# Decode attention beside a feed-forward branch, one core: the first weight load is split by partitions

## The chip, the cores and the metric

The kernel runs on one core of a Trainium2 chip. The metric is the device time of one execution in microseconds. The kernel before took 695.85 us (median of 3 runs, 695.55 to 696.01). One more execution was recorded by the hardware profiler; all rows shown are of that one.

## The reference

Two tokens (batch 2, one query position, width 640) go through two branches. Branch A is attention over a cache of 4096 positions with 32 heads of 128; branch B is a feed-forward layer of width 1728 with SiLU. A gate of each token mixes them. All is float32.

```python
def _A_ref(x, k_cache, v_cache, wq, wo):
    B, Sq, D = x.shape          # 2, 1, 640
    H, Dh = 32, 128             # caches: (2, 32, 4096, 128)
    q = (x @ wq).reshape(B, Sq, H, Dh).transpose(0, 2, 1, 3)
    scores = jnp.einsum("bhqd,bhkd->bhqk", q, k_cache) * (Dh ** -0.5)
    p = softmax(scores, axis=-1)
    o = jnp.einsum("bhqk,bhkd->bhqd", p, v_cache)
    return o.transpose(0, 2, 1, 3).reshape(B, Sq, H * Dh) @ wo

def _B_ref(x, w1, w2):          # w1 (640, 1728), w2 (1728, 640)
    h = silu(jnp.einsum("bsd,df->bsf", x, w1))
    return jnp.einsum("bsf,fd->bsd", h, w2)

g = sigmoid((x * gate_w).sum(-1, keepdims=True))
out = g * _A_ref(...) + (1 - g) * _B_ref(...)
```

## The kernel before

**Storage.** Three large areas of SBUF, the slabs `v`, `b` and `a`, hold 64 KB in each of the 128 partitions. Everything that is read in bulk passes through them: the weights of branch B and `wq` at the start, then the K and V caches, then `wo`.

**The start.** The queue of SyncE (SP in the profile) issues every transfer. Its first ones are, in this order: `w1` into slab `a` (line 303: 128 partitions, each with five whole rows of `w1`, 34,560 contiguous bytes), `x` into the tile `xs` (8 partitions), `gate` into `xs` (4 partitions), `w2` into slab `v`, `wq` into the end of `v` and all of `b` (lines 304 to 312), and a small store to the output. The issue of `x` waits for the memset of `oP_xs` on GpSimd (line 302). VectorE turns `x` and the gate row (line 420), makes a few small tiles, and then multiplies `w1` by `x` in ten steps over 1728 columns (lines 443 and 446); the first of them reads slab `a` and so waits for `w1`. TensorE sums over partitions (line 458), the SiLU follows, TensorE multiplies by `w2` (line 533) and then computes all queries from `wq` (line 608).

**The main part.** Batch and heads give 16 items of four heads each. An item has one K slab and one V slab of 8.4 MB. K goes to `a` and `b` in turn, V to `v`. For each item VectorE (line 676, columns 0 to 67) and GpSimd (line 670, the other 60) multiply K by the query in place, VectorE reduces (line 686), ScalarE takes the exponentials (line 715), TensorE multiplies them with V (line 766). The load of a K slab waits until the slab's reader before it is done, and the load of a V slab until the values of the item before are summed. The first K load (line 470, `load_k(0)`) goes into slab `a` and waits for the last VectorE step on `w1`; the first V load (line 656) and the second K load (line 657) wait for the matmuls on `wq` (line 608).

**The end.** `wo` is loaded in six pieces behind the last V slab; TensorE multiplies piece after piece (lines 556 and 586) and one store writes the result.

**Order and waits.** Every operation names the pieces it reads and writes (`part("a", 0)` is piece 0 of slab `a`, `part("a")` all eight), and the class `Flow` derives the semaphore waits from them. Each transfer has a semaphore of its own unless it names another.

Of the kernel before, what the change touches and what calls it, by code (L numbers as in the profile page):

```python
# [158 lines left out]
def gated_decode(nc, x, kc, vc, wq, wo, w1, w2, gate, out):  # L159
    P = 128  # L160
    B, H, SK, DH = kc.shape
    D = x.shape[2]
    F = w1.shape[1]
    J = D // P
# [26 lines left out]
    f = Flow(nc)  # L191
# [11 lines left out]
    slab = {n: slabs[:, k * SLAB : (k + 1) * SLAB] for k, n in enumerate("vba")}  # L203

    def part(n, *ks):
        return [f"{n}.{k}" for k in (ks or range(8))]
# [77 lines left out]
    def load_wo(g):  # L284
# [15 lines left out]


    f.op("POOL", lambda: G_.memset(oP_xs, 0.0), writes=["oP", "xs"])
    f.dma("SP", slab["a"][:, : J * F], w1.rearrange("(p j) f -> p (j f)", j=J), writes=part("a"))
    f.dma("SP", xs[0:P:HB, :], x.rearrange("b s (c n) -> (s c) b n", c=Q), reads=["xs"], writes=["xs0"])
    f.dma("SP", xs[HB // 2 : P : 32, :], gate.rearrange("(c n) -> c n", c=Q), reads=["xs"], writes=["xs1"])
    f.dma(
# [3 lines left out]
        writes=part("v", 0),  # L310
# [10 lines left out]
        writes=["ident"],  # L321
# [13 lines left out]
        writes=["block"],  # L335
# [7 lines left out]
        writes=["fold"],  # L343
# [5 lines left out]
        writes=["sel"],  # L349
# [5 lines left out]
        writes=["half"],  # L355
# [10 lines left out]
        writes=["pick"],  # L366
# [5 lines left out]
        writes=["own"],  # L372
# [5 lines left out]
        writes=["side"],  # L378
# [7 lines left out]
        writes=["spread"],  # L386
# [5 lines left out]
        writes=["mask"],  # L392
    )
    f.op("DVE", lambda: V.memset(join, 0.0), writes=["join"])
    for e in range(2):
# [7 lines left out]
            writes=["join"],  # L403
        )
        for t in (at, at + 32):
# [4 lines left out]
                writes=["join"],  # L410
# [11 lines left out]
        writes=["xt"],  # L422
# [6 lines left out]
        writes=["gx"],  # L429
# [7 lines left out]
    for b in range(B):  # L437
        for j in range(J):
# [13 lines left out]
                writes=[f"hsum{b}"],  # L452
            )

    def mm_hr():
# [19 lines left out]
        writes=["ps_o"],  # L475
# [8 lines left out]
        writes=["gc"],  # L484
# [7 lines left out]
    for e in range(2):  # L492
# [4 lines left out]
            writes=[f"spaced{e}"],  # L497
# [9 lines left out]
        writes=["he"],  # L507
    )
    for e in range(2):
# [6 lines left out]
            writes=[f"seq{e}"],  # L516
# [126 lines left out]
    for u in range(2):  # L643
        for b in range(B):
# [8 lines left out]
                writes=[f"qall{u}{b}"],  # L653
# [199 lines left out]
    for i in range(N + 1):  # L853
        j = i - 1
# [98 lines left out]
```

## Time and profile before

| what | value |
|---|---|
| median of 3 runs | 695.85 us (695.55 to 696.01) |
| the profiled execution, its own time | 695.71 us |
| its span, first to last instruction | 694.2 us |
| VectorE, GpSimd, TensorE, ScalarE busy | 507.5, 265.6, 211.4, 40.0 us |
| read from HBM | 298.26 MB |

The profiled execution's own time is 1.5 us above its span; the rest lies ahead of the first and behind the last instruction. SPq is the queue of SyncE, from which the transfers are issued; "to landing" is the time from an issue to the end of its transfer. In the rows of a time window the engines' busy times come first, then the granted TensorE clock, the busy share of the 16 DMA engines and the bytes per time. A packet is counted with its whole size where it begins, so that the share of a short window can pass 1.

### The profile page before, as it was taken

How to read it: one execution, taken by the hardware profiler on the slowest of the kernel's cores; microseconds unless marked ns; L12 is line 12 of the kernel's file. 1: busy time of each engine (PE TensorE's matmuls, PEld its weight loads, DVE VectorE, ACT ScalarE, POOL GpSimd, SP SyncE). 2: the span in 40 equal slices, each digit the busy share in tenths (PEclk: the TensorE clock that was granted, in tenths of full speed). 3: DMA queues.
4: the chain of work that ended last, by engine and by line, in shares of the span. 5: the costliest groups of instructions: out<-in, count | busy, mean ns of one | idle time of the engine just before them, and what ended most of it. 6: DMA issues, size and time to landing. Idle time of an engine off the chain costs nothing. (4 is left out here: it accounts for less than half of the span.)

```text
span 694.2 us, 3593 instructions
## 1 busy us (share of the span) xinstructions
PE 211.4 (30%) x1440; PEld 72.5 (10%) x1440; DVE 507.5 (73%) x269; ACT 40.0 (6%) x152; POOL 265.6 (38%) x26
## 2 busy tenths in 40 slices
PE   0074032151331405060412306060503315050657
PEld 0032010010110101020100101010100101010113
DVE  3810958898989596886959596986959595977811
ACT  0001010101010101010010101010000101010000
POOL 1000808191726090815335180906244270907100
PEclk9998556565565757575665757575655757575689
DMA  9999999999999999999999999999999999999997
GB/s 383 430 446 450 430 427 424 423 457 438 427 430 423 430 461 427 434 423 423 438 457 427 430 423 427 464 430 430 423 423 461 434 430 427 423 438 457 427 408 326
DMA packets 6209, 298.33 MB, mean 430 GB/s; under 512 B 672, under 2 KB 700, under 8 KB 956
## 3 DMA queue, kind: packets, MB, share of 16 engines
q1 hardware_dynamic: 6204, 298.27, 99.4%
q8 instruction: 2, 0.03, 0.0%
q14 instruction: 3, 0.02, 0.0%
HBM read 298.26 MB, written 0.01 MB: 430 GB/s over the span
## 5 line engine op out<-in xcount | busy, mean ns | idle before, releaser
L670 POOL TENSOR_TENSOR slabs<-slabs,qsb 128x7680 f32<-128x7680 f32 x16 | 262.3, 16396 | 378.7 <-DMA slabs<-in_A_k_cache_dram 347.8
L686 DVE TENSOR_REDUCE s<-slabs 128x68 f32<-128x8704 f32 (+1 forms) x32 | 276.3, 8676 | 0.0
L766 PE MATMUL ps<-slabs,pz 128*32 128x512 f32 x1024 | 146.2, 735 | 345.2 <-PEq L145 338.2
L676 DVE TENSOR_TENSOR slabs<-slabs,ps 128x8704 f32<-128x8704 f32 x16 | 147.5, 9218 | 108.5 <-DMA slabs<-in_A_k_cache_dram 108.4
L766 PEld LDWEIGHTS ps<-slabs,pz 128*32 128x32 f32 x1024 | 39.5, 132 | 438.6 <-issue 431.6
L715 ACT ACTIVATE pz<-s,nb 32x128 f32<-32x128 f32 x64 | 25.4, 398 | 556.5 <-PE ps L766 363.2
L804 PE MATMUL ps<-osb,pick 128*128 128x512 f32 x32 | 20.4, 724 | 58.9 <-PEq L145 58.0
L818 DVE TENSOR_REDUCE row<-ps 64x128 f32<-64x512 f32 x16 | 10.9, 682 | 23.3 <-PE ps L804 23.3
L788 DVE SCALAR_TENSOR_TENSOR osb<-ps,rg,own 128x512 f32<-128x512 f32 x16 | 12.0, 748 | 21.4 <-PE ps L766 21.2
L618 PE MATMUL ps<-qall,spread 128*128 (+1 forms) x32 | 7.4, 319 | 35.3 <-PEq L145 34.5
L446 DVE SCALAR_TENSOR_TENSOR slabs<-slabs 128x1728 f32<-128x1728 f32 x8 | 16.1, 2019 | 0.3
L458 PE MATMUL ps<-slabs,xz_col 128*32 128x432 f32 x16 | 3.1, 928 | 33.2 <-DVE slabs L446 33.2
L804 PEld LDWEIGHTS ps<-osb,pick 128*128 128x128 f32 x32 | 5.4, 211 | 73.0 <-issue 71.2
L715 ACT ACTIVATION_READ_ACCUMULATOR pz<-s,nb 32x1 f32 x64 | 11.8, 184 | 0.0
L618 PEld LDWEIGHTS ps<-qall,spread 128*128 128x128 f32 x32 | 6.9, 224 | 44.9 <-issue 43.2
L533 PE MATMUL ps<-slabs,seq 128*32 128x320 f32 x54 | 10.3, 545 | 3.7 <-DVE seq L512 3.7
L825 DVE STREAM_TRANSPOSE ps<-row 64x256 f32<-64x256 f32 x16 | 10.3, 642 | 0.6
L608 PE MATMUL ps<-slabs,xz_col 128*32 128x512 f32 x80 | 9.8, 593 | 0.0
L891 DVE COPY slabs<-ps 128x160 f32<-128x160 f32 x1 | 0.3, 325 | 12.2 <-PE ps L586 12.2
L556 PE MATMUL ps<-slabs,oP_xs 128*32 128x320 f32 x96 | 8.8, 433 | 1.4 <-DMA slabs<-in_A_wo_dram 1.4
L740 PE MATMUL ps<-rs,fold 128*128 128x1 f32 x32 | 6.1, 260 | 2.3 <-PEq L145 2.1
L740 PEld LDWEIGHTS ps<-rs,fold 128*128 128x128 f32 x32 | 5.7, 222 | 5.0 <-issue 3.5
(63 smaller groups left out, 71.9 us busy)
## 6 DMA issues: line engine op xcount, KB each, us to landing
slabs<-in_A_wq_dram SPq DMA_DIRECT2D x1, 10240.0 KB, 44.5
slabs<-in_B_w_dram SPq DMA_DIRECT2D x2, 4320.0 KB, 17.0
slabs<-in_A_wo_dram SPq DMA_DIRECT2D x1, 5120.0 KB, 21.5
slabs<-in_A_wo_dram SPq DMA_DIRECT2D x2, 1280.0 KB, 25.4
slabs<-in_A_wo_dram SPq DMA_DIRECT2D x1, 1600.0 KB, 30.1
slabs<-in_A_wo_dram SPq DMA_DIRECT2D x1, 640.0 KB, 31.1
slabs<-in_A_wo_dram SPq DMA_DIRECT2D x1, 320.0 KB, 31.4
slabs<-in_A_k_cache_dram SPq DMA_DIRECT2D x16, 47.8
```

The lines of the kernel that those rows point to most:

```text
L446: lambda b=b, j=j, at=at: V.scalar_tensor_tensor(hsum[:, b, :], w1t[:, j, :], at, hsum[:, b, :], op0=ALU.mult, op1=ALU.add)
L533: last = T_.matmul(early[to : to + 32, :], seq[:, k : k + 2, :].rearrange("p k z -> p (k z)"), slab[n][:, k * HD : (k + 1) * HD], start=(k ...
L618: return T_.matmul(ps_q[:, :DH], spread, qall.rearrange("p h b d -> p (h b) d")[:, i, :], start=True, stop=True,)
L670: lambda: G_.tensor_mul(k[:, CV:, :], k[:, CV:, :], qsb[:, None, :].to_broadcast([P, C - CV, DH])),
L676: lambda: V.tensor_mul(k[:, :CV, :], k[:, :CV, :], ps_q[:, None, :DH].to_broadcast([P, CV, DH])),
L686: lambda c0=c0, c1=c1: V.reduce_sum(Ss[i % 2][:, c0:c1], k[:, c0:c1, :], axis=AX.X),
L715: last = S_.activation(pz[lo:hi, :, 4 * q : 4 * q + 4], s[lo:hi].rearrange("p (g c) -> p g c", c=4), AF.Exp, bias=nb[lo:hi], scale=SCALE, ...
L740: lambda *_: T_.matmul(ps_t[:, :1], fold.rearrange("p a q c -> p (a q c)"), rs, start=True, stop=True),
L766: last = T_.matmul(ps_v[32 * q : 32 * q + 32, :], pz[:, gr, :], v[:, gr, :], start=(gr < 4), stop=(gr >= NG - 4),)
L788: lambda: V.scalar_tensor_tensor(osb, ps_v.rearrange("p (c d) -> p c d", d=DH), rg, own[:, :, None].to_broadcast([P, 4, DH]), op0=ALU.mult ...
L804: lambda *_: T_.matmul(ps_o, pick, osb.rearrange("p c d -> p (c d)"), start=True, stop=True),
L818: lambda: V.reduce_sum(row, ps_o[:64].rearrange("p (c d) -> p d c", d=DH), axis=AX.X),
```

## The change

The load of `w1` becomes two loads of the same bytes: the first takes partitions 0 to 63, the second partitions 64 to 127. Each partition still receives one run of 34,560 bytes. The first load is entered as the writer of piece 0 of slab `a`, the second as the writer of pieces 1 to 7. Both are issued from the same queue, one behind the other and ahead of `x`. The first VectorE step on `w1` reads all pieces, and so waits for two semaphores where it waited for one.

```diff
     f.op("POOL", lambda: G_.memset(oP_xs, 0.0), writes=["oP", "xs"])
-    f.dma("SP", slab["a"][:, : J * F], w1.rearrange("(p j) f -> p (j f)", j=J), writes=part("a"))
+    w1_rows = w1.rearrange("(p j) f -> p (j f)", j=J)
+    f.dma("SP", slab["a"][: P // 2, : J * F], w1_rows[: P // 2], writes=part("a", 0))
+    f.dma("SP", slab["a"][P // 2 :, : J * F], w1_rows[P // 2 :], writes=part("a", *range(1, 8)))
     f.dma("SP", xs[0:P:HB, :], x.rearrange("b s (c n) -> (s c) b n", c=Q), reads=["xs"], writes=["xs0"])
```

## The prediction

> **What bounds the kernel now.** I read the busy table first, then the DMA rows, then the chain of waits, and last the windows of the start.
>
> ```profile
> PE 211.4 (30%) x1440; PEld 72.5 (10%) x1440; DVE 507.5 (73%) x269; ACT 40.0 (6%) x152; POOL 265.6 (38%) x26
> DMA  9999999999999999999999999999999999999997
> GB/s 383 430 446 450 430 427 424 423 457 438 427 430 423 430 461 427 434 423 423 438 457 427 430 423 427 464 430 430 423 423 461 434 430 427 423 438 457 427 408 326
> q1 hardware_dynamic: 6204, 298.27, 99.4%
> HBM read 298.26 MB, written 0.01 MB: 430 GB/s over the span
> DMA 4%; PE 2%; SPq 0%; issue 0%; DVE 0%
> DMA slabs<-in_A_wo_dram 4%; PE ps L766 1%; PE ps L586 0%; SPq L69 0%; DVE slabs L891 0%
> ```
>
> No compute engine is near full; VectorE, the busiest, stands at 73%. The 16 DMA engines are busy for 99.4% of the span, in each of the 40 slices. The chain of waits follows only the last 46 us, but in those, too, the largest piece is a transfer (`wo`, 4%). The waits say the same for the main part: GpSimd, which takes up each K slab, sits idle until the slab has landed.
>
> ```profile
> POOL slabs L670 <- DMA slabs<-in_A_k_cache_dram: 347.8, 14, 64.4
> ...
> 0.00:1.70 1.70, 0.00 (x0) 0.00 (x0) 0.17 (x1) 0.97 (x1) 1.17 (x5) 1.00 0.00 0
> ...
> 67.00:667.00 600.00, 166.63 (x1052) 54.35 (x1052) 479.30 (x219) 35.33 (x143) 262.33 (x16) 0.62 1.00 433
> ```
>
> The first window is empty, and the one from 67 to 667 us, in which nearly all K and V slabs pass, has a DMA share of 1.00 at 433 GB/s. So the kernel is one long stream of 298 MB, always with something queued, and its time is bytes by rate plus a head and a tail. Two things follow. Time that the stream loses at the start is not won back later: the idle share is 0.6%, 4.2 us, and 1.7 us of that is ahead of the first packet. And moving bytes earlier or later within the stream gains nothing.
>
> **The change part by part.** The first question is how long `w1` takes now.
>
> ```profile
> 0.74 0.38 SPq L69 DMA_DIRECT2D slabs<-in_B_w_dram  x1
> 1.85 0.73 SPq L69 DMA_DIRECT2D oP_xs<-in_A_x_dram  x1
> 2.63 0.56 SPq L69 DMA_DIRECT2D oP_xs<-in_gate_w_dram  x1
> 3.23 0.43 SPq L69 DMA_DIRECT2D slabs<-in_B_w_dram  x1
> 3.71 0.43 SPq L69 DMA_DIRECT2D slabs<-in_A_wq_dram  x1
> slabs<-in_B_w_dram SPq DMA_DIRECT2D x1, 4320.0 KB, 13.1
> 1.70:12.50 10.80, 0.00 (x0) 0.00 (x0) 3.21 (x17) 0.32 (x1) 2.07 (x6) 1.00 1.02 410
> 13.48:33.20 19.72, 0.00 (x0) 0.00 (x0) 19.09 (x15) 0.00 (x0) 0.00 (x0) 1.00 1.00 431
> ```
>
> `w1` is issued at 0.74 us and lands 13.1 us later, at 13.84. It is 4320 KB, that is 4.424 MB. The window 1.70 to 12.50 moves 410 GB/s x 10.8 us = 4.43 MB: all of `w1` and next to nothing else. So `w1` holds the stream for about 10.8 us; at the settled rate of the window behind it, 431 GB/s, it would be 4.424 / 0.431 = 10.27 us, and 0.5 us are the run-up of the first packets.
>
> *The second issue.* An issue of this kind takes 0.38 to 0.43 us. SP is free from 1.12 us, and its next issue, `x`, begins only at 1.85 us, behind the memset on GpSimd:
>
> ```profile
> 0.73 1.09 POOL L302 MEMSET oP_xs<- 128x1192 f32 x1 [0.29 <-POOLq L943]
> ```
>
> 0.43 us go into that gap of 0.73 us: cost nothing. Without that cover it would move the issues of `x`, gate, `w2` and `wq` by 0.43 us, and their packets would still wait behind `w1` until about 12.5 us; nothing again.
>
> *The second wait.* The first VectorE step on `w1` (line 443) now waits for two loads. Ahead of it on VectorE stands the transposition at line 420, which waits for the gate row:
>
> ```profile
> 13.75 0.46 DVE L420 STREAM_TRANSPOSE slabs<-oP_xs 128x160 f32<-128x160 f32 x1 [7.72 <-DMA oP_xs<-in_gate_w_dram]
> 14.62 1.11 DVE L443 TENSOR_SCALAR slabs<-slabs 128x1728 f32<-128x1728 f32 x1
> 25.01 8.18 DVE L446 SCALAR_TENSOR_TENSOR slabs<-slabs 128x1728 f32<-128x1728 f32 x4
> 33.22 0.34 SPq L69 DMA_DIRECT2D slabs<-in_A_k_cache_dram  x1
> slabs<-in_A_wq_dram SPq DMA_DIRECT2D x1, 10240.0 KB, 44.5
> ```
>
> The gate row is queued behind both halves, so it stays the last to come, or lies within tenths of it. What is queued behind line 443 is the ten steps that end at 33.2 us and release the first K load at 33.22. That load then waits in the queue until `wq` has landed at 3.71 + 44.5 = 48.2 us: 15 us of cover. A second wait costs 0 within it; with the cover gone it would be some tenths.
>
> *The transfers themselves.* No load of this trace fills only half the partitions, apart from the few KB of `x` and gate, so the price must be bounded. **Low end, 0:** the rate belongs to the 16 engines, both halves are spread over all of them, and 64 partitions load as fast as 128. **High end:** the rate belongs to the destination. All bulk loads fill 128 partitions, at 431 / 128 = 3.37 GB/s for each of them; if a partition cannot take more, 64 take 215.5 GB/s. The halves then go one after the other, since one queue feeds both: 4.424 / 0.2155 = 20.5 us, against 10.8 now, +9.7 us. With the run-up doubled too (half of 410) it is 21.6, +10.8 us. I take +9.7. The rows cannot tell the ends apart by number, because full engines and full destinations come together in every one of them. What turns me to the high end is that the loads of this kernel differ in source, in row length (34,560 bytes here, 64 KB for K) and in slab, and yet run at 431 to 433 GB/s: what they share is the span of 128 partitions, and that is what the change halves. The run-up is counted once, since at half rate the destination, not the start of the packets, would be late.
>
> [...] No run here shows a 64-partition load yet.
>
> *What is late next.* The stream as a whole moves back by 9.7 us: `wq` lands near 58 us, and the VectorE steps end near 43. The next issues wait for the matmuls on `wq`:
>
> ```profile
> 59.51 0.33 SPq L69 DMA_DIRECT2D slabs<-in_A_v_cache_dram  x1
> slabs<-in_A_k_cache_dram SPq DMA_DIRECT2D x1, 35.0
> ```
>
> The first K slab is the last thing queued then; it lands at 33.22 + 35.0 = 68.2 us, 8.7 us behind the issue of V. Both ends of that cover move together, so no hole opens, and none of the delay is hidden.
>
> **Sum:** 0 + 0 + 9.7 on the profiled execution's own 695.71 us gives 705.4. The median of the runs is 0.14 us above that execution, which I leave out.
>
> **The rivals.** *The engines set the rate (not slower).* The place is the DMA engine: it moves its rows as fast to any 64 partitions as to 128, and the halves follow without a gap. For it: the DMA share is 1.00, so the engines are never seen waiting. Against it: the share tells that packets were under way, not what set their pace. Time: 695.7, less at most the 0.53 us of run-up, which two loads might smooth: 695.2 to 696.2. It decides if a 64-partition load passes at about 430 GB/s.
>
> *The engines drift apart.* The destination limits, but of the engines that compete for the same partitions half win. They finish the first load at full rate and start on the second while the losers are still on the first. Half a load's time, about 4.9 us, is then overlapped: +4.9, 700.6. For it: nothing makes 16 engines keep step. Against: it needs a lasting preference, and equal sharing gives none.
>
> *The change does not split what it says.* If the two loads went to two disjoint sets of eight engines, they would run beside each other at full rate. Place and price are those of the first rival, 0, and I count them together.
>
> *The delay is hidden.* The DMA share of 1.00 from 67 to 667 us leaves no idle time to take it up. I give it nothing of its own.
>
> **How the numbers follow.** Destination limit, one half after the other: 0.78, 705.4, own range 704.3 to 706.8. Drift: 0.09, 700.6. No price: 0.10, near 695.7. Left over: 0.03, of which 0.02 is a gain that I cannot name. A change of 0.2% is 1.4 us, about what a measurement of this kernel can tell. A gain of that size would need more than the whole run-up, 0.53 us. So faster 0.02, same 0.10, slower 0.88. The range reaches down to the drift, 700.5, and up to the doubled run-up with some tenths, 707.0; outside lies the case without a price, and little else.
>
> **What would show it.** In the changed profile:
> - the first of the 40 slices falls from 383 to some 215 GB/s, and the second stays partly low (`w1` ends near 22 us), while all later ones stay at 420 to 460;
> - the first half lands near 13 us and the second near 23 us; line 420 starts near 23.4 instead of 13.75, the first K load is issued near 43, the first V load near 69;
> - from there to the end each event stands 9 to 10 us later, at the same spacing, with a DMA share of 1.00.
>
> The prediction is wrong at its only real term if line 420 still starts near 14 us (no price), or near 18 to 19 us (drift). It is wrong about the stream if line 420 is 9 us late and the end is not.

## The result and the profile after

The changed kernel took **707.18 us** (median of 6 runs, 706.59 to 707.91) against 695.81 us of the kernel before: a ratio of 1.0164, with a 95% interval of 1.0151 to 1.0177. It is 11.4 us slower. A second set of runs on another occasion gave 706.71 us against 695.85, ratio 1.0154 (1.0137 to 1.0171), 10.9 us. The forecast was 705.4, with a range up to 707.0: the sign and the place were right, the size was too small by 1.3 to 1.8 us, and the median lies 0.18 us above the range.

The page of the kernel after: the span, the DMA row of its 40 slices, the bytes per time in each, and the queue.

```profile
span 705.4 us, 3595 instructions
DMA  9999999999999999999999999999999999999997
GB/s 192 347 446 455 427 420 432 450 420 424 465 420 424 457 424 427 431 450 420 427 461 420 424 465 420 424 439 442 420 431 457 420 424 465 420 424 450 431 406 319
q1 hardware_dynamic: 6220, 298.28, 99.3%
```

The DMA engines look as busy as before, 99.3% against 99.4%. What changed is in the row below: 192 GB/s in the first slice where there were 383, 347 in the second where there were 430, and the old rates from the third slice on. A busy engine is not a fast one.

Next the windows of the start and of the main part (the last two numbers are the DMA share and the GB/s), then the first VectorE steps and three rows of the SyncE queue.

```profile
1.70:12.50 10.80, 0.00 (x0) 0.00 (x0) 3.21 (x17) 0.31 (x1) 2.07 (x6) 1.00 1.00 211
12.50:23.00 10.50, 0.00 (x0) 0.00 (x0) 0.00 (x0) 0.00 (x0) 0.00 (x0) 1.00 1.00 207
23.00:33.00 10.00, 0.00 (x0) 0.00 (x0) 7.84 (x9) 0.00 (x0) 0.00 (x0) 1.00 1.03 426
77.00:677.00 600.00, 165.96 (x1052) 54.33 (x1052) 479.38 (x219) 35.32 (x143) 262.38 (x16) 0.63 1.00 434
```

```profile
24.99 0.46 DVE L422 STREAM_TRANSPOSE slabs<-oP_xs 128x160 f32<-128x160 f32 x1 [18.96 <-DMA oP_xs<-in_gate_w_dram]
...
25.86 1.12 DVE L445 TENSOR_SCALAR slabs<-slabs 128x1728 f32<-128x1728 f32 x1
```

```profile
0.73 1.23 SPq L69 DMA_DIRECT2D slabs<-in_B_w_dram  x2
2.01 0.66 SPq L69 DMA_DIRECT2D oP_xs<-in_A_x_dram  x1
...
44.47 0.34 SPq L69 DMA_DIRECT2D slabs<-in_A_k_cache_dram  x1
70.01 0.33 SPq L69 DMA_DIRECT2D slabs<-in_A_v_cache_dram  x1
```

For as long as `w1` is loaded the stream moves 207 to 211 GB/s, half of its usual rate. At 23 us it is back at 426. The transposition that waits for the gate row starts at 24.99 us instead of 13.75, 11.24 us late; the first K load is issued 11.25 us late and the first V load 10.5. In the main part the stream runs at 434 GB/s with a share of 1.00, as before. So the whole loss stands in the first 24 us, and the rest of the program carries it to the end: the span is 11.2 us longer.

### The profile page after: what moved, and what is told of

The parts are those of the page before. It is cut to its first block, busy times and chain, and to the rows that moved or that the text cites. A ratio compares the mean times of both kernels' runs of the same rounds, so it can differ in the third digit from the quotient of the medians.

```text
span 705.4 us, 3595 instructions
## 1 busy us (share of the span) xinstructions
PE 210.9 (30%) x1440; PEld 72.5 (10%) x1440; DVE 507.6 (72%) x269; ACT 40.0 (6%) x152; POOL 265.6 (38%) x26
## 3 DMA queue, kind: packets, MB, share of 16 engines
q1 hardware_dynamic: 6220, 298.28, 99.3%
## 5 line engine op out<-in xcount | busy, mean ns | idle before, releaser
L820 DVE TENSOR_REDUCE row<-ps 64x128 f32<-64x512 f32 x16 | 10.9, 682 | 23.3 <-PE ps L806 23.3
L893 DVE COPY slabs<-ps 128x160 f32<-128x160 f32 x1 | 0.3, 325 | 11.2 <-PE ps L588 11.2
```

The source lines that it names most:

```text
L820: lambda: V.reduce_sum(row, ps_o[:64].rearrange("p (c d) -> p d c", d=DH), axis=AX.X),
```

## The experiments

Each is the kernel before with the edit shown. In all but the run with the K slab the load of `w1` is the line replaced, and `w1_rows` is defined as in the change. The theories are told with the expectations.

**Two loads, but by columns.** Is it the splitting?

```diff
+    cut = J * F // 2
+    f.dma("SP", slab["a"][:, :cut], w1_rows[:, :cut], writes=part("a", 0))
+    f.dma("SP", slab["a"][:, cut : J * F], w1_rows[:, cut:], writes=part("a", *range(1, 8)))
```

> The first weights again in two loads, but each takes all 128 partitions and half of each row (17,280 bytes). Theory D (the destination: a load whose partitions all lie in one half of SBUF, 0 to 63 or 64 to 127, is received at 204 GB/s, the rate of the changed kernel's packets, 34,560 bytes in about 2.7 us on each of 16 engines): each load fills both halves, so the time is that of the kernel before, 695.5 to 696.3 us, and the gate row lands near 13.8 us. Theory S (splitting costs: a second load, or fewer rows for an engine in each load): about 707 us, gate row near 25 us.

Measured: 695.98 us, ratio 0.9996 (0.9986 to 1.0006). Within that interval (-1.0 to +0.4 us) splitting alone is free; theory S falls. The run-up was not smoothed by it either: the window 1.70 to 12.50 us has 405 GB/s, where the kernel before has 410.

**Four loads of 32 partitions.** Is it a rate of each partition, as the prediction had it?

```diff
+    for k, (lo, hi) in enumerate(((0, 32), (32, 64), (64, 96), (96, 128))):
+        f.dma("SP", slab["a"][lo:hi, : J * F], w1_rows[lo:hi], writes=part("a", *((k,) if k < 3 else range(3, 8))))
```

> The first weights in four loads of 32 contiguous partitions. Theory D: each lies in one half and is received at 204 GB/s, so the four take 4.424 MB / 0.204 = 21.7 us as the two halves do: 706.5 to 708 us. Theory P (a rate for each partition, 204 / 64 = 3.2 GB/s, as the prediction had it): 32 partitions take 102 GB/s, 43 us for the four, 32 us more than before: about 728 us. Theory S: three splits, 11 us each, about 730 us. Theory P and S part in the columns run.

Measured: 706.34 us, ratio 1.0147 (1.0128 to 1.0166). A stretch within the four loads:

```profile
3.95:20.00 16.05, 0.00 (x0) 0.00 (x0) 1.82 (x16) 0.00 (x0) 0.05 (x1) 1.00 1.00 207
```

32 partitions are received as fast as 64 (207 GB/s here, 205 to 211 in the changed kernel), so a partition took twice of what it had there. Theory P falls, and with it the prediction's mechanism.

**The middle first.** Three loads, of partitions 32 to 95, 0 to 31 and 96 to 127, by the same loop over other bounds.

> The first weights in three loads: partitions 32 to 95, 0 to 31, 96 to 127. Theory D: the first load has 32 partitions in each half and runs at 431 GB/s (5.1 us), the other two at 204 GB/s (5.4 us each), 16 us against 10.8: +5 to +6, 700.5 to 702 us. Theory P: 10.8 + 10.8 + 10.8 us, +22, about 718 us. Theory S: two splits, about 718 us.

Measured: 702.54 us, ratio 1.0092 (1.0073 to 1.0111), +6.5 us: a little above what theory D gave, and far from the two others. The rows of the first load show the same thing directly; here its issue with its time to landing, in the run with the middle first:

```profile
slabs<-in_B_w_dram SPq DMA_DIRECT2D x1, 2160.0 KB, 9.5
```

and that of the first load in the changed kernel, of as many partitions and bytes:

```profile
slabs<-in_B_w_dram SPq DMA_DIRECT2D x1, 2160.0 KB, 13.4
```

64 contiguous partitions across the middle land 3.9 us sooner than 64 at the bottom. By the rates of theory D it would be 5.7 us (10.8 - 5.1); why it is less is not shown. The stretch in which only packets of the middle load begin has nearly the full rate:

```profile
3.90:7.80 3.90, 0.00 (x0) 0.00 (x0) 1.88 (x16) 0.00 (x0) 0.11 (x1) 1.00 0.99 425
```

**A K slab in halves.** Does the price grow with the bytes, and away from the start?

```diff
-    load_k(0)
+    users = f.users(part("a"))
+    k_rows = run_of(kflat, 0)
+    f.dma("SP", slab["a"][: P // 2], k_rows[: P // 2], writes=part("a"), after=users)
+    f.dma("SP", slab["a"][P // 2 :], k_rows[P // 2 :], writes=["a.high"], after=users)
```

The two products of the first item wait for `a.high` too.

> The first weights in one load as before, but the first K slab (8.39 MB) in two loads of 64 contiguous partitions. Theories D and P: 8.39 / 0.204 = 41.1 us against 8.39 / 0.433 = 19.4, +21.7 us: about 717.5 us, since the stream is full there as well. Theory S as a fixed price for a split: about 707 us. If the start alone were slow (run-up, first packets): no change, 696 us.

Measured: 718.16 us, ratio 1.0314 (1.0295 to 1.0334), +22.1 us. Twice the bytes, twice the price. The window that lies within this slab, 36 us long, gives the rate better than the short load of `w1` can:

```profile
50.00:86.00 36.00, 9.57 (x84) 4.89 (x82) 0.00 (x0) 2.57 (x5) 0.00 (x0) 0.66 0.99 204
```

and the same window of the kernel before:

```profile
50.00:86.00 36.00, 9.96 (x88) 5.27 (x80) 17.61 (x2) 2.58 (x5) 16.39 (x1) 0.68 0.99 426
```

204 GB/s is not half of the 431 to 433 of the settled stream, but 5% less than half. The engines show the same share, 0.99, at either rate.

**The halves on two queues.** The second half goes through ScalarE's queue; the bounds in `spans` count ScalarE's operations, of which there is now one more.

```diff
+    f.dma("SP", slab["a"][: P // 2, : J * F], w1_rows[: P // 2], writes=part("a", 0))
+    f.dma("ACT", slab["a"][P // 2 :, : J * F], w1_rows[P // 2 :], writes=part("a", *range(1, 8)))
...
-    spans = {"ACT": (14, 34), "DVE": (100, 220), "PE": (len(f.ops["PE"]) - NP * PR - 1, len(f.ops["PE"]))}
+    spans = {"ACT": (15, 35), "DVE": (100, 220), "PE": (len(f.ops["PE"]) - NP * PR - 1, len(f.ops["PE"]))}
```

> The two halves of the changed kernel, but the second is issued by ScalarE's queue, at the same time as the first by SyncE's. Theory D (each half of SBUF takes 204 GB/s, the two together twice that): each of the 16 engines now has rows of both halves at hand. If the engines take the two queues in step, all write the same half at the same moment and nothing is won: 706 to 708 us. If they are out of step by half, both halves fill at once: 696 us. I expect something between, nearer to the first: 703 to 707. Theory Q (the price is that one queue serves the halves in order, with a gap between them): 696 us.

Measured: 706.77 us, ratio 1.0162 (1.0133 to 1.0192). A window of this run, 1.7 to 12.5 us, and a longer stretch within its two loads:

```profile
1.70:12.50 10.80, 0.00 (x0) 0.00 (x0) 2.81 (x17) 0.93 (x1) 2.15 (x6) 1.00 1.07 234
4.25:19.38 15.13, 0.00 (x0) 0.00 (x0) 1.17 (x9) 0.00 (x0) 0.00 (x0) 1.00 1.00 219
```

and a stretch within the first load of the changed kernel:

```profile
4.20:12.30 8.10, 0.00 (x0) 0.00 (x0) 1.62 (x12) 0.00 (x0) 0.00 (x0) 1.00 1.00 205
```

219 GB/s instead of 205, both at a share of 1.00; the 234 of the short window goes with a share of 1.07. The two loads are open together (issued at 0.74 and 0.73 us, they land 23.2 and 20.6 us later), and the rate is 14 GB/s higher, not doubled. In the median the gain cannot be told from nothing. The spans of three of the four executions are 704.3 to 704.5 us, about 1 us below the 705.2 to 705.5 of the changed kernel; that of the fourth is 708.5. Theory Q falls. Whether the engines took the two queues in step, as the expectation weighed, no view shows.

**Even and odd partitions.** Two loads of 64 partitions, spread over all of SBUF.

```diff
+    for k in range(2):
+        f.dma("SP", slab["a"][k::2, : J * F], w1_rows[k::2], writes=part("a", *((0,) if k == 0 else range(1, 8))))
```

> Two loads of 64 partitions each, the even ones and then the odd ones. Theory D in its plain form (what counts is how many of a load's partitions lie in each half of SBUF; here 32 and 32): 695.5 to 697.5 us, the gate row near 14 us. Theory N (a load of 64 partitions is slow whichever they are): 706 to 708 us. Something between would say that which engine writes which partition counts too.

Measured: 696.17 us, ratio 1.0006 (0.9997 to 1.0016); line 422 starts at 13.99 us. A stretch within the two loads:

```profile
3.88:11.58 7.70, 0.00 (x0) 0.00 (x0) 1.89 (x16) 0.00 (x0) 0.12 (x1) 1.00 1.00 431
```

Two loads of 64 partitions, each spread over all of SBUF, ran at 431 GB/s, where two loads of 64 contiguous ones had 205 to 211, and the time shows no price. The number of partitions in a load is not what made the difference.

**The second half later.** It is issued behind `x` and gate.

```diff
+    f.dma("SP", slab["a"][: P // 2, : J * F], w1_rows[: P // 2], writes=part("a", 0))
     f.dma("SP", xs[0:P:HB, :], x.rearrange("b s (c n) -> (s c) b n", c=Q), reads=["xs"], writes=["xs0"])
     f.dma("SP", xs[HB // 2 : P : 32, :], gate.rearrange("(c n) -> c n", c=Q), reads=["xs"], writes=["xs1"])
+    f.dma("SP", slab["a"][P // 2 :, : J * F], w1_rows[P // 2 :], writes=part("a", *range(1, 8)))
```

> The changed kernel with its second half issued behind x and gate instead of ahead of them. The price of the transfers stays under theory D: 706 to 708 us. If the later first packet of the changed kernel (2.11 us against 1.74 in the span) came from the second issue right behind the first, it is back at 1.74 us here and the time some 0.4 us shorter than the changed kernel's; if it belongs to a first load of 64 partitions, it stays at 2.1. The gate row now lands near 14 us, and VectorE then waits at its first step on the weights until about 25 us.

Measured: 706.95 us, ratio 1.0156 (1.0139 to 1.0172). The wait of VectorE moves from the gate row to the weights:

```profile
14.67 0.46 DVE L422 STREAM_TRANSPOSE slabs<-oP_xs 128x160 f32<-128x160 f32 x1 [9.05 <-DMA oP_xs<-in_gate_w_dram]
...
24.89 1.12 DVE L445 TENSOR_SCALAR slabs<-slabs 128x1728 f32<-128x1728 f32 x1 [9.27 <-DMA slabs<-in_B_w_dram]
```

and the time stays. Which of the two VectorE waits for is of no account; the bytes in the stream are. The window 1.74 to 2.10 us is still without a packet (0 GB/s), so the late first packet is not the work of a second issue close behind.

**The changed kernel once more.**

> The changed kernel once more, beside the others on one chip: 706.5 to 708 us, gate row near 25 us, first slice of the span at some 190 GB/s. It tells how much of the differences of a few tenths between such runs is chance.

Measured: 706.71 us; line 422 at 24.82 us, a span of 705.3. Half a microsecond lies between the two medians of the same kernel, though its spans agree (705.2 to 705.5 us on both occasions). So the quarters (706.34) and the two queues are not shown by their medians to be better than the halves. By the spans the quarters are some 0.4 us shorter, at 704.9 to 705.0 us.

**Eighths, contiguous and spread.** "One half of SBUF" fits all runs so far: 64 and 32 contiguous partitions within one half had 205 and 207 GB/s, sets with as many in each half 425 and 431. Two ways of loading 16 partitions at a time ask whether the half alone counts.

```diff
+    for k in range(8):
+        lo, hi = 16 * k, 16 * k + 16
+        f.dma("SP", slab["a"][lo:hi, : J * F], w1_rows[lo:hi], writes=part("a", k))
```

> The first weights in eight loads of 16 contiguous partitions. Theory H (only the half of SBUF counts: any set of partitions within 0 to 63 or within 64 to 127 takes 204 GB/s): 21.7 us for all, 706.5 to 708 us. [...]

```diff
+    for k in range(8):
+        f.dma("SP", slab["a"][k::8, : J * F], w1_rows[k::8], writes=part("a", k))
```

> Eight loads of 16 partitions again, but load k takes partitions k, k+8, k+16 and so on to k+120, 8 of them in each half of SBUF. Theory H: full rate, 696 to 697 us. [...]

Measured: contiguous 723.03 us, ratio 1.0366 (1.0284 to 1.0448); spread 707.22 us, ratio 1.0142 (1.0061 to 1.0223). The seven runs of the kernel before beside them scatter from 695.58 to 712.55 us around a median of 695.80, hence the wide intervals. By the medians the prices are 27.2 and 11.4 us. A stretch of 24 us within the contiguous eighths:

```profile
9.90:33.95 24.05, 0.00 (x0) 0.00 (x0) 0.00 (x0) 0.00 (x0) 0.00 (x0) 1.00 1.01 115
```

and the window 12.5 to 23 us of the spread ones:

```profile
12.50:23.00 10.50, 0.00 (x0) 0.00 (x0) 0.00 (x0) 0.00 (x0) 0.00 (x0) 1.00 0.98 204
```

16 contiguous partitions are received at 115 GB/s, a little over a quarter of the 431 of the even and odd sets; 16 with a step of 8, half of them in each half of SBUF, at 204. Theory H falls in both: it had 204 GB/s for the contiguous ones and the full rate for the spread ones. The time of the contiguous eighths follows from their rate: 4.424 MB / 0.115 = 38.5 us, 27.7 more than the 10.8 before, beside the 27.2 of the medians. All eight loads are queued early in that time (their issues end at 4.46 us); whether two of them overlapped in the stretch is not shown. So the rate goes neither with the half of SBUF alone nor with the number of partitions alone: about a quarter for 16 contiguous ones (115 GB/s), about a half for 32 and 64 contiguous ones within one half (207, 205) and for 16 with a step of 8 (204), and nearly all or all of it for the middle (425) and for the even and odd sets (431). What sets these rates is not shown.

Two things were not varied alone. The rows of `w1` in memory go with the partitions in every run; since the middle load reads an unbroken stretch as long as that of a half, and has 425 GB/s where the half has 205, the length of the stretch is not the cause, but other effects of the source address are not excluded. And no view shows which engine writes which partition.

## Why the prediction was right, and where it was wrong

**The stream bounds the kernel: right.** A loss of 11.24 us at the gate row is a loss of 11.2 us in the span. Nothing took it up, the main part ran on at 434 GB/s, and the K slab in halves shows the same far from the first load.

**The engines set the rate (0.10): wrong.** 204 against 426 GB/s with the same engines and the same share. The objection was sound: the DMA share says that packets are under way, not what sets their pace.

**The loads go to disjoint engines: wrong.** The rate fell by half, where two sets of engines side by side would have kept it, and the share of 1.00 in that time says that all 16 engines had packets under way.

**The engines drift apart (0.09): did not happen.** The rate is 211 and then 207 GB/s through both halves. Drift would have brought the full rate for a part of that time: 4.9 us of the load would have been overlapped.

**The failed step is the high end of the transfers**: "if a partition cannot take more, 64 take 215.5 GB/s". The mechanism was false. Partitions took about twice the 3.37 GB/s that the prediction allowed them: the quarters put 207 GB/s into 32 partitions (6.5 each), the even and odd sets 431 into 64 (6.7 each), and the contiguous eighths 115 into 16 (7.2 each). What the runs showed in its place is that the rate goes with which partitions a load has: 64 of them were received at 205 to 211 GB/s within one half of SBUF, at 425 across the middle and at 431 alternating. What lies behind this is not shown. For contiguous halves the false mechanism gives a factor of two, and the measured factor is near two (431 against 204), so that the sum came out near was luck. A forecast for quarters by that mechanism would have been 22 us too high (728 against 706.34).

**Two sizes were off**, which takes the time past the range; the term of 9.7 us measured 11.24 at the gate row:
- The rate of contiguous halves is 204 GB/s (the K slab) and not 215.5. 4.424 MB / 0.204 = 21.7 us, where the prediction had 20.5: 1.2 us. The stretch of the changed kernel shown with the two queues has 205. Half of the settled rate was taken for granted; what was measured is another 5% below that half, and why is not shown.
- The first packets come later, which the sum did not have. The window 1.74 to 2.10 us, of before and then of after:

```profile
1.74:2.10 0.36, 0.00 (x0) 0.00 (x0) 0.00 (x0) 0.28 (x1) 0.23 (x2) 1.00 4.39 1152
```

```profile
1.74:2.10 0.36, 0.00 (x0) 0.00 (x0) 0.00 (x0) 0.27 (x1) 0.22 (x2) 1.00 0.00 0
```

Some 0.4 us are lost there. Together, 21.7 - 10.8 + 0.4 = 11.3 us, beside 11.24 at the gate row and 10.9 to 11.4 in the medians. The bound of 10.8 us for a doubled run-up came close to the right size for another reason than the one given.

**The second issue: free, as said, but longer than said.** The two issues take 1.23 us together, not 0.8, and `x` is issued at 2.01 us instead of 1.85. The minimum, median and maximum of the issues' durations in ns, for the three loads of `w1` and `w2`:

```profile
L69 SPq DMA_DIRECT2D slabs<-in_B_w_dram x3: 435/571/603, 0.7 to 3.3; - x3
```

The halves take 571 and 603 ns, `w2` over 128 partitions 435.

**The second wait: free, as said.** The step on `w1` starts 0.87 us behind the start of the transposition, before (14.62 - 13.75) and after (25.86 - 24.99). The covers moved together as forecast: the first K load is issued at 44.47 us (forecast near 43), the first V load at 70.01 (near 69).

## What to carry to other kernels

Where a kernel is one stream of transfers, ask of each load which partitions it covers. Here the split by columns, with all partitions in each load, and the split by alternating partitions cost nothing that the medians show (695.98 and 696.17 us, beside 696.02 and 695.85 of the kernel before). Contiguous blocks within one half of SBUF halved the rate for 32 or 64 partitions (207 and 205 GB/s) and brought it near a quarter for 16 (115). A spread set was not enough by itself: 16 partitions with a step of 8 were received at 204 GB/s, half of the rate. Read bytes per time beside the DMA share, since the share stayed at 0.99 while the rate fell from 426 to 204 GB/s. And when a bound rests on a mechanism that the trace cannot tell from another, work out a second case in which the two differ before the rate of one is taken.

## What was not expected of the hardware

The first packet came some 0.4 us later in the changed kernel, and it did so with other sets of 64 partitions in the first load too. In the run with even and odd ones the same window is empty as well:

```profile
1.74:2.10 0.36, 0.00 (x0) 0.00 (x0) 0.00 (x0) 0.27 (x1) 0.22 (x2) 1.00 0.00 0
```

So it is with the middle first and with the second half later (0 GB/s in both). The window has 1152 GB/s in the kernel before, 624 in the run by columns and 864 in the quarters, whose first load has 32 contiguous partitions. In the run with even and odd ones this is the only price left, and the time, +0.3 us with an interval that holds zero, cannot show it. The delay goes with the issue of the first load: 0.60 us in the changed kernel and with the second half later, 0.38 us in the kernel before. Why some sets take longer to issue is open.
